# Linear attention and a gated MLP on one core: weight loads over 128 partitions, batch loads moved to SyncE, first batch rebuilt

## The chip, the cores and the metric

The kernel runs on one core of one Trainium2 chip. The metric is the time of one execution in device microseconds (us), as the median over runs. The span of a profile is about 1.8 us shorter than the time of the same run.

PE is the tensor engine, DVE the vector engine, ACT the scalar engine, POOL the GpSimd, SP (SyncE) the engine that here only issues DMAs. "ACTq" and "SPq" are the queues in which ACT and SP issue.

## The reference, cut to what matters

```python
batch, n_heads, seq, head_dim = (8, 8, 576, 64)          # q, k, v, float32
n_tokens, d_model, d_ff = (4608, 512, 2048)              # w_in 512 x 2048, w_out 2048 x 512, beta 2048

def phi(x, c, s):                                        # c, s: cos and sin of the position
    r = np.maximum(x, 0.0)
    return np.concatenate([r * c, r * s], axis=-1)
q_p, k_p = phi(q, cos_w, sin_w), phi(k, cos_w, sin_w)
kv = np.einsum('bhsf,bhsd->bhfd', k_p, v)
z = np.sum(k_p, axis=2)
num = np.einsum('bhsf,bhfd->bhsd', q_p, kv)
den = np.einsum('bhsf,bhf->bhs', q_p, z)[..., None] + 1e-06
x = num / den                                            # then the heads side by side: 4608 x 512
h = x @ w_in
out = (h * (1.0 / (1.0 + np.exp(-beta * h)))) @ w_out
```

## The kernel before

The MLP works on nine chunks of 512 tokens. Each chunk has 32 slots: 16 of `h_group` (four matmuls with w_in, then a Silu on ACT), then 16 of `o_part` (four matmuls with w_out). The attention of the next batch is worked in between the slots, so PE should never pause. Only the attention of batch 0 stands alone at the start, and all weights arrive in that time and during chunk 0.

The partition of a w_in row follows from how the attention output is turned: partition 64 jj + d of contraction block (jp, g) must hold row 256 jp + 128 jj + 64 g + d of w_in. So the 128 partitions of one block take two groups of 64 neighbouring rows, 128 rows apart. The kernel before loads each group by itself:

```python
w_in_v = moe_w_in.rearrange("(jp jj g d) f -> jj d jp g f", jp=2, jj=2, g=2)
def load_w(kind, i, f0=0, f1=512):
    ...
    for jj in range(2):                  # 64 partitions per load
        for jp in range(2):
            nc.sync.dma_start(
                out=st[jj * HP : (jj + 1) * HP, 2 * jp : 2 * jp + 2, f0:f1],
                in_=w_in_v[jj, :, jp, :, i * 512 + f0 : i * 512 + f1])
...
    for slot in range(32):               # chunk 0
        ...
    for name in "qvk":
        load_raw(2, name, eng=nc.scalar)
    for c in range(1, NTC):
        if c + 2 < B:
            for name in "qvk":
                load_raw(c + 2, name, eng=nc.scalar)     # batch loads issued by ACT
        units = att_units(c + 1) if c + 1 < B else []
```

## Time and profile before

| | before |
|---|---|
| time, median of 3 | 348.11 us (345.81 to 348.89) |
| span of the profile | 346.3 us |
| PE busy | 88% |
| mean granted clock of PE | 0.962 |
| first MLP matmul / first of chunk 1 | 25.7 / 70.1 us |

The profile page of before: the span in 40 slices of 8.7 us. The digits are tenths of busy share (PE), of full clock (PEclk) and of the 16 DMA engines' time (DMA).

```profile
PE   5469958828999899979996999899999999999994
...
PEclk9789989976999999999998999999999999999998
DMA  7999990389618942595149706960640251032022
GB/s 276 266 217 256 389 377 12 88 306 389 228 37 154 316 163 50 112 305 204 39 105 253 276 18 129 273 251 17 133 112 3 49 113 30 0 70 53 0 60 61
```

From about slice 11 on PE is nearly always busy. The loose time is mostly in the first 90 us. The DMA engines are full in slices 2 to 6, but at 217 GB/s in slice 3 and at 389 in slice 5. The windows view of before gives for each stretch (us) its length, then PE, PEld, DVE, ACT and POOL busy with counts, then the granted clock, the DMA share, GB/s:

```profile
12.00:32.00 20.00, 14.34 (x193) 8.86 (x195) 12.39 (x29) 9.29 (x16) 4.15 (x3) 0.83 1.03 212
35.00:40.00 5.00, 5.00 (x25) 2.13 (x23) 2.13 (x5) 3.90 (x6) 0.00 (x0) 1.00 1.05 388
```

The w_in loads run in the first stretch, loads of all 128 partitions in the second. Both have the engines full; the loads into 64 partitions move 212 GB/s. The Trainium skill, "SBUF — State Buffer", section "Door 1: The DMA port swizzle (why [64,N] ≈ [32,N])", says that 64 partitions reach only 8 of the 16 ports; its asymptote for them, 8 × 27.2 GB/s, is close to the 212 that this trace shows.

The PE timeline of before, MLP matmuls at the starts of chunks 0 and 1. The columns are start and duration in us, engine, line, operation, count, and in brackets the idle time before and what ended it:

```profile
25.67 14.49 PE L339 MATMUL ps<-xt,win 128*128 128x512 bf16 x64 [0.67 <-ACT xt L321]
...
70.07 1.89 PE L339 MATMUL ps<-xt,win 128*128 128x512 bf16 x8 [0.46 <-ACT xt L321]
78.83 12.75 PE L339 MATMUL ps<-xt,win 128*128 128x512 bf16 x44 [6.88 <-ACT g_t L343]
```

PE idles 6.9 us in chunk 1 because it waits for ACT (`g_t` is the Silu). What ACT did is in the timeline of all engines in that stretch:

```profile
71.37 0.79 ACTq L78 DMA_DIRECT2D raw_q<-in_q_dram  x1
72.19 3.08 ACTq L78 DMA_DIRECT2D raw_v<-in_v_dram  x1
75.31 2.74 ACTq L78 DMA_DIRECT2D raw_k<-in_k_dram  x1
...
77.14 9.66 SPq L241 DMA_TRANSPOSE qt<-qb  x1
78.09 1.27 ACT L343 ACTIVATE g_t<-ps,beta 128x512 bf16<-128x512 f32 x2 [7.59 <-issue]
```

ACT issues six batch loads in a row, two of which hold its queue for about 3 us each, and only then the Silu.

### The profile page before, as it was taken

To read this page: it belongs to the slowest core of one execution; us is meant where nothing else is said; L and a number is where in the kernel's file an instruction comes from. 1 tells how busy PE (TensorE), PEld (TensorE's weight loads), DVE (VectorE), ACT (ScalarE), POOL (GpSimd) and SP (SyncE) were. 2 spreads that over 40 slices of the span, in tenths; PEclk is the share of its full clock that TensorE was granted. 3 is DMA by queue.
4 is the path that set the end of the run, shared out by engine and by line. 5 is a ranking of instruction groups with operands and counts; after the bars stand their busy time and mean duration, and the time that the engine had idled before them with its cause. 6 is when DMAs were issued, how large, how long until landed. Compare 5 with 4: busy or idle time off the path is not lost.

```text
span 346.3 us, 5863 instructions
## 1 busy us (share of the span) xinstructions
PE 306.4 (88%) x2363; PEld 146.2 (42%) x2390; DVE 125.9 (36%) x332; ACT 136.2 (39%) x209; POOL 73.5 (21%) x83
## 2 busy tenths in 40 slices
PE   5469958828999899979996999899999999999994
PEld 2354434413444345434542444345444544444441
DVE  3871479517239024802480058114902400000000
ACT  6437501505611661256113721463166127516711
POOL 2520000310233601342131503800370120000000
PEclk9789989976999999999998999999999999999998
DMA  7999990389618942595149706960640251032022
GB/s 276 266 217 256 389 377 12 88 306 389 228 37 154 316 163 50 112 305 204 39 105 253 276 18 129 273 251 17 133 112 3 49 113 30 0 70 53 0 60 61
DMA packets 50986, 53.60 MB, mean 155 GB/s; under 512 B 31232, under 2 KB 32272, under 8 KB 50960
## 3 DMA queue, kind: packets, MB, share of 16 engines
q1 hardware_dynamic: 38736, 24.65, 28.4%
q10 hardware_dynamic: 9536, 21.24, 16.7%
q0 software_dynamic: 2688, 7.34, 9.1%
q8 instruction: 18, 0.29, 0.4%
q14 instruction: 8, 0.07, 0.1%
HBM read 36.71 MB, written 9.44 MB: 133 GB/s over the span
## 4 chain that ended last, share of the span: by engine, by line
PE 68%; DMA 17%; ACTq 5%; DVE 3%; issue 2%; SPq 2%; ACT 1%; POOL 1%; POOLq 0%; DVEq 0%
PE ps L352 32%; PE ps L339 28%; DMA w_stage<-in_moe_w_out_dram 8%; PE ps L279 5%; ACTq L78 5%; DMA qt<-qb 4%; DMA raw_k<-in_k_dram 3%; DMA w_stage<-in_moe_w_in_dram 2%; PE ps L256 2%; SPq L97 1%; DVE wout L114 1%; DVE qs L218 1%; ACT g_t L343 1%; SPq L78 1%; POOL qs L218 1%
## 5 line engine op out<-in xcount | busy, mean ns | idle before, releaser
L339 PE MATMUL ps<-xt,win 128*128 128x512 bf16 x576 | 138.4, 387 | 15.4 <-ACT g_t L343 14.3
L352 PE MATMUL ps<-wout,g_t 128*128 128x512 bf16 x550 | 126.4, 380 | 2.5 <-issue 1.6
L343 ACT ACTIVATE g_t<-ps,beta 128x512 bf16<-128x512 f32 x144 | 98.4, 687 | 61.2 <-PE ps L339 47.7
L339 PEld LDWEIGHTS <-win 128*128 128x128 bf16 x576 | 56.3, 99 | 93.4 <-issue 35.9
L352 PEld LDWEIGHTS <-g_t 128*128 128x128 bf16 x576 | 54.6, 98 | 64.8 <-issue 1.2
L366 POOL DMA_DIRECT2D out_dram<-o_sb x56 | 36.2, 650 | 167.2 <-ACT o_sb L362 167.1
L362 ACT COPY o_sb<-ps 128x512 f32<-128x512 f32 x35 | 20.5, 586 | 108.8 <-PE ps L352 108.8
L271 DVE CAST kv<-ps 64x130 bf16<-64x130 f32 x60 | 17.5, 292 | 87.8 <-PE ps L256 86.8
L218 POOL TENSOR_TENSOR qs<-qt,tanr 128x1152 bf16<-128x1152 bf16 x12 | 28.3, 2378 | 35.7 <-DMA qt<-qb 26.9
L360 DVE COPY o_sb<-ps 128x256 f32<-128x256 f32 x1 | 0.4, 425 | 65.5 <-ACT o_sb L359 65.5
L295 DVE TENSOR_TENSOR xs<-ps,rden 128x768 bf16<-128x768 f32 (+1 forms) x27 | 23.4, 868 | 0.9
L279 PE MATMUL ps<-kv,qt 128*64 128x130 bf16 x288 | 21.2, 229 | 1.3 <-DVE kv L271 1.3
L279 PE MATMUL ps<-kv,qs 128*64 128x130 bf16 x288 | 20.6, 228 | 1.1 <-DVE qs L218 0.6
L279 PEld LDWEIGHTS <-qt 128*64 128x64 bf16 x288 | 16.4, 114 | 11.3 <-issue 10.5
L256 PE MATMUL ps<-vb,rk 64*64 64x130 bf16 x576 | 12.7, 235 | 7.6 <-ACT rk L194 4.0
L214 DVE TENSOR_SCALAR vb<-raw_v,cos 128x256 bf16<-128x256 f32 x63 | 17.1, 348 | 3.4 <-DMA raw_v<-in_v_dram 3.4
L279 PEld LDWEIGHTS <-qs 128*64 128x64 bf16 x288 | 16.7, 113 | 1.4 <-DVE qs L218 0.7
L214 DVE TENSOR_SCALAR vb<-raw_v,sin 128x256 bf16<-128x256 f32 x63 | 17.1, 349 | 0.0
L290 DVE TENSOR_TENSOR den<-ps,eps 128x12 f32<-128x12 f32 (+1 forms) x27 | 4.5, 168 | 32.1 <-PE ps L279 32.1
L256 PEld LDWEIGHTS <-rk 64*64 64x64 bf16 x576 | 10.1, 116 | 12.3 <-issue 6.4
L196 DVE TENSOR_SCALAR qb<-raw_q 128x1152 bf16<-128x1152 f32 x15 | 10.7, 753 | 8.1 <-DMA raw_q<-in_q_dram 8.1
L236 ACT COPY qt<-ps 128x640 bf16<-128x640 bf16 (+1 forms) x8 | 4.9, 640 | 22.1 <-PE ps L230 17.8
(51 smaller groups left out, 79.5 us busy)
## 6 DMA issues: line engine op xcount, KB each, us to landing
out_dram<-o_sb POOLq DMA_DIRECT2D x56, 128.0 KB, 2.9
raw_q<-in_q_dram ACTq DMA_DIRECT2D x6, 1152.0 KB, 7.7
raw_v<-in_v_dram ACTq DMA_DIRECT2D x6, 1152.0 KB, 10.5
raw_k<-in_k_dram ACTq DMA_DIRECT2D x6, 1152.0 KB, 12.3
w_stage<-in_moe_w_out_dram SPq DMA_DIRECT2D x4, 1024.0 KB, 14.1
w_stage<-in_moe_w_in_dram SPq DMA_DIRECT2D x12, 256.0 KB, 9.0
out_dram<-o_sb SPq DMA_DIRECT2D x16, 128.0 KB, 2.4
raw_q<-in_q_dram SPq DMA_DIRECT2D x2, 576.0 KB, 4.5
```

What stands on the lines that cost most here:

```text
L78: (eng or nc.sync).dma_start(out=raw_tile(b, name)[:, js].rearrange("q j n d -> q j (n d)"), in_=src.rearrange("(j g) (p n) d -> (g p) j ( ...
L214: nc.vector.tensor_scalar(vb[:, n, :, cs, 0:D], rv[:, :, n, :], scalar1=t[:, n : n + 1], scalar2=None, op0=ALU.mult)
L218: eng.tensor_tensor(dst.rearrange("q n (g p) -> q n g p", g=2), src.rearrange("q n (g p) -> q n g p", g=2), tanr[:, n0:n1].unsqueeze(2).to ...
L256: nc.tensor.matmul(t[jj * HP : (jj + 1) * HP, g], lhsT=rk[hs, n, 2 * jp + jj, :], rhs=vb[hs, n, 2 * jp + jj].rearrange("q s e -> q (s e)") ...
L271: nc.vector.tensor_copy(o, a)
L279: nc.tensor.matmul(ps[gs_, bank, i * 2 * E : (i + 1) * 2 * E], lhsT=(qt, qs)[cs][:, jp, n, gs_], rhs=kv[:, g, jp, cs, :], start=(cs == 0), ...
L295: nc.vector.tensor_tensor(xs[:, jps[0] : jps[-1] + 1, 3 * t : 3 * t + 3].rearrange("q s n (j d) -> q s (n j) d", j=2), nv[:, :, :, :, 0:D] ...
L339: nc.tensor.matmul(h_ps, lhsT=win[jt // 4][:, mi, (jt % 4) * P : (jt % 4 + 1) * P], rhs=xt[:, jp, :, g * HP : (g + 1) * HP], start=(mi == ...
L343: nc.scalar.activation(g_t, h_ps, AF.Silu, scale=beta[:, jt : jt + 1])
L352: nc.tensor.matmul(o_ps, lhsT=gs[c, jt][:, tt * P : (tt + 1) * P], rhs=wout[jt // 4][:, jt % 4, :], start=(jt == 0), stop=(jt == JT - 1))
L362: nc.scalar.copy(o_sb, o_ps)
L366: eng.dma_start(out=out_v[bb, n], in_=o_sb[hf * HP : (hf + 1) * HP, :])
```

## The change

It has three parts. First, each w_in load covers all 128 partitions, to use all ports. Second, SyncE issues the batch loads, after the query transposes, so that ACT is free. Third, the attention of batch 0 is rebuilt (scaling, relu, evictions and divisions spread over DVE, ACT, POOL and PE, fewer and larger copies), and the slots of batch 1's work in chunk 0 are shifted. The diff, cut to its core:

```diff
-    w_in_v = moe_w_in.rearrange("(jp jj g d) f -> jj d jp g f", jp=2, jj=2, g=2)
+    w_in_v = moe_w_in.rearrange("(jp jj g d) f -> jp g jj d f", jp=2, jj=2, g=2)
...
-        for jj in range(2):
-            for jp in range(2):
-                nc.sync.dma_start(
-                    out=st[jj * HP : (jj + 1) * HP, 2 * jp : 2 * jp + 2, f0:f1],
-                    in_=w_in_v[jj, :, jp, :, i * 512 + f0 : i * 512 + f1])
+        for mi in range(MI):
+            nc.sync.dma_start(out=st[:, mi], in_=w_in_v[mi // 2, mi % 2, :, :, i * 512 : (i + 1) * 512])
...   (batch 0: v_scale, k_relu, kv_take, x_rden, x_mul, x_mul_act: cut)
     early = {
...
-        21: lambda: (kv_mm(1, 0, 6), kv_mm(1, 1, 6), kv_take(1, 0, 6), kv_take(1, 1, 6)),
-        22: lambda: (q_relu(1, 0), q_relu(1, 1)),
-        23: lambda: cast_w("out", 3),
-        24: lambda: q_turn_pe(1, 0, 4),
-        25: lambda: q_turn_pe(1, 1, 6),
+        22: lambda: (kv_mm(1, 0, 6), kv_mm(1, 1, 6), kv_take((0, 1), 6), q_relu(1, 0), q_relu(1, 1),
+                     q_turn_pe(1, 0, 4)),
+        23: lambda: (q_turn_pe(1, 1, 6), cast_w("out", 2)),
+        24: lambda: cast_w("out", 3),
...
+        def load_next():
+            for name in "qvk":
+                if b + 1 < B:
+                    load_raw(b + 1, name)
-            (0, lambda: (q_relu(b, 0), q_relu(b, 1))),
+            (0, lambda: (q_relu(b, 0), q_relu(b, 1), q_turn_dma(b), load_next())),
-            (1, lambda: q_turn_dma(b)),
...
-    for name in "qvk":
-        load_raw(2, name, eng=nc.scalar)
     for c in range(1, NTC):
-        if c + 2 < B:
-            for name in "qvk":
-                load_raw(c + 2, name, eng=nc.scalar)
```

The shapes of one w_in load, as built: before, source 64 × 2 × 512 (or 256) into 64 partitions; after, source 2 × 64 × 512 into 128 partitions. The first quarter, which before loads in halves, comes whole (16 loads instead of 20).

## The prediction

> **What bounds the kernel now.** The page gives PE 88% busy over a 346.3 us span, and the chain of waits is 68% PE. The steady part is bound by the tensor engine: the timeline shows about 32 us of matmuls per 512-token chunk. The loose time is at the start. By the PE timeline the first MLP matmul starts at 25.7 us and the second chunk's at 70.1 us, 44 us later where a chunk without stalls takes 32 to 33. The chain shows DMA there: w_in until 25.6 us, w_out until 51.8 us. Then ACT issues batch loads: 7 us of ACTq in the chain at 70 to 77 us (PE idles 6.9 us, released by g_t), and 1.5 to 3 us of ACTq at the start of each of chunks 2 to 5.
>
> **What the change gains.** SyncE issuing the batch loads frees ACT: I estimate 7 to 9 us in chunk 1 and 1.2 to 2 us in each of chunks 2 to 5, about 14 us. The rebuilt first batch could start the MLP some 4 us earlier, if its weights are there. Fewer and larger kv copies and transposes cost or gain nothing on the bound engine later.
>
> **What it costs: the w_in loads.** Before, each load's source pattern starts with 64 rows; the slices view shows all DMA engines busy at 200 to 240 GB/s while these run (12 to 30 us), against about 392 GB/s for the 128-partition loads. The change means to gain that factor. But in the new loads the source is a pattern of 2 x 64 x 512 (the two row groups are 128 rows apart and do not merge) against 128 partitions. The Trainium skill, "DMA: Bandwidth & Descriptors", section "Why a DMA increments its semaphore by 16 and not by 1", says a DMA from SyncE runs on the largest number of engines up to 16 that divides the outermost non-one dimension of both patterns, and takes the lowest-numbered ones. That is 2 here, the same two for all 16 loads. No load of the trace before has such a shape, so this is untested here.
>
> Estimate from the trace: 392 GB/s over 16 engines is 24.5 GB/s each (a 2 KB packet took 84 ns where ports were free). 4.19 MB over two engines takes 86 us, against about 19 us before. The first batch's loads end near 12 us, so the four w_in chunks land near 34, 55, 77 and 98 us. w_out and batch 1 wait behind them on those two engines: about 101 us for the first w_out, 106, 109 and 112 us for v, k, q, 115 and 118 us for the last w_out. Then follow the scaling of v (4.9 us), relu, the kv matmuls, the query transposes and divisions, about 21 us as before. Chunk 1 starts near 135 us instead of 70.
>
> **Sum.** 348.1 + 65 - 14 = about 399 us; I say 398 us, range 380 to 418 us. Faster by over 2%: 0.08; within 2%: 0.02; slower: 0.90.
>
> **What would show it.** w_in loads landing about 5.4 us apart; DMA busy share near 1/8 and about 50 GB/s from 12 to 98 us; PE idle in long pieces before 98 us, ended by DMA of w_stage through the casts; chunk 1 starting at 125 to 145 us; no 7 us ACTq wait after it; chunks of 32 to 34 us. A first MLP matmul near 35 us, not 25, would show the loads outweigh the rebuilt first batch.
>
> **What would make it wrong.** If the loads spread over all 16 engines, they would finish by about 23 us and the result would be near 325 us, faster by 6%. If a lone engine moves more than 24.5 GB/s, up to 10 us less; if a lone engine is slower, 10 us or more above.

## The result, and the profile after

| | before | after |
|---|---|---|
| time, median of 4 runs | 347.72 us (345.81 to 348.89) | 393.0 us (392.2 to 393.72) |
| ratio | | 1.1308 (1.125 to 1.1366) |
| span / mean granted clock | 346.3 us / 0.962 | 390.9 us / 0.899 |
| first MLP matmul / first of chunk 1 | 25.7 / 70.1 us | 34.1 / 133.8 us |
| chunks 1 to 8 and the end | 276.2 us | 257.1 us |

The last row is the span less the start of chunk 1. A ratio here is the mean time of one kernel's fast runs over that of the other's of the same rounds, so it is not quite the ratio of the medians.

The profile page of after, in slices of 9.8 us:

```profile
PE   8535032230868999999999999999999999999994
...
PEclk9755658585696999999999999999999999999999
DMA  8311111129993494890693397189064034013013
GB/s 277 130 50 52 51 51 50 50 56 292 387 389 116 94 310 152 186 377 9 131 313 151 70 237 289 22 188 365 21 136 94 2 80 90 1 27 82 1 32 77
```

For seven slices, from 20 to 88 us, the DMA engines are one or two tenths busy and move 50 to 56 GB/s, while PE mostly stands still. The windows view of after puts the share for 14 to 80 us at 0.13, about 2 of 16:

```profile
14.00:80.00 66.00, 23.58 (x169) 12.33 (x169) 8.90 (x14) 9.92 (x20) 2.02 (x2) 0.59 0.13 51
```

The PE timeline of after shows chunk 0 in four pieces, one for each quarter of w_in. Each waits 10 to 18 us for the cast of a quarter that just landed. The last line is the start of chunk 1:

```profile
34.08 5.96 PE L368 MATMUL ps<-xt,win 128*128 128x512 bf16 x16 [9.97 <-POOL win L105]
55.05 5.71 PE L368 MATMUL ps<-xt,win 128*128 128x512 bf16 x16 [15.02 <-DVE win L107]
75.86 5.54 PE L368 MATMUL ps<-xt,win 128*128 128x512 bf16 x16 [15.10 <-DVE win L107]
99.51 5.67 PE L368 MATMUL ps<-xt,win 128*128 128x512 bf16 x16 [18.10 <-DVE win L107]
...
133.80 12.06 PE L368 MATMUL ps<-xt,win 128*128 128x512 bf16 x52 [0.61 <-ACT xt L351]
```

The chain of waits of after, in the stretch from 14 to 35 us, shows loads 5.1 us apart on SP. Columns are start, duration, what.

```profile
14.03 5.07 SPq L96
...
19.14 5.08 SPq L96
...
24.26 5.08 SPq L96
```

One load is 262,144 bytes; in 5.1 us that is 51 GB/s, or 25.7 GB/s for each of two engines. SP does not wait for an earlier load here (its waits view from 4 to 82 us is empty): the issue itself takes 5.1 us, and what holds it is not shown. Two to three loads are outstanding: when the first four had landed and their cast began at 33.0 us, six had been issued and the seventh was being issued.

The w_in loads also hold up what follows them. The chain has v of batch 1 issued at 87.5 us and landing 18.8 us later:

```profile
87.49 18.81 DMA raw_v<-in_v_dram
```

The packed trace holds the time of every update of a load's semaphore. Of the sixteen for this v, fourteen came from 98.9 to 99.7 us and the last two at 106.2 and 106.3 us: its share on the two slow engines stands behind the last w_in loads and two w_out loads.

### The profile page after: what moved, and what is told of

Same layout as the page of the kernel before. It is cut to its first block, busy times and chain, and to the rows that moved or that the text cites. A ratio compares the mean times of both kernels' runs of the same rounds, so it can differ in the third digit from the quotient of the medians.

```text
span 390.9 us, 5820 instructions
## 1 busy us (share of the span) xinstructions
PE 314.0 (80%) x2398; PEld 148.4 (38%) x2398; DVE 117.5 (30%) x279; ACT 137.7 (35%) x215; POOL 74.0 (19%) x83
## 4 chain that ended last, share of the span: by engine, by line
PE 68%; SPq 22%; DMA 5%; DVE 3%; issue 1%; ACT 0%; ACTq 0%; DVEq 0%
PE ps L381 31%; PE ps L368 30%; SPq L96 19%; DMA raw_v<-in_v_dram 5%; PE ps L280 4%; PE ps L256 2%; SPq L93 2%; DVE vb L213 1%; SPq L78 1%; PE ps L228 0%; DVE qs L216 0%; DVE kv L272 0%; DVE rk L190 0%; DVE qb L190 0%; ACT g_t L372 0%
## 5 line engine op out<-in xcount | busy, mean ns | idle before, releaser
L368 PE MATMUL ps<-xt,win 128*128 128x512 bf16 x576 | 142.4, 396 | 58.9 <-DVE win L107 48.2
L381 PE MATMUL ps<-wout,g_t 128*128 128x512 bf16 x576 | 131.8, 383 | 1.9 <-DVE wout L111 1.9
L368 PEld LDWEIGHTS <-win 128*128 128x128 bf16 x576 | 57.1, 101 | 140.1 <-DVE win L107 49.7
L272 DVE CAST kv<-ps 64x520 bf16<-64x520 f32 (+1 forms) x16 | 10.6, 664 | 80.2 <-PE ps L256 80.0
L107 DVE CAST win<-w_stage 128x2048 bf16<-128x2048 f32 x3 | 3.7, 1226 | 71.1 <-DMA w_stage<-in_moe_w_in_dram 71.1
L298 DVE TENSOR_TENSOR xs<-ps,rden 128x768 bf16<-128x768 f32 x21 | 20.1, 957 | 0.7
L293 DVE TENSOR_TENSOR den<-ps,eps 128x12 f32<-128x12 f32 x21 | 3.6, 171 | 38.1 <-PE ps L280 38.1
L256 PE MATMUL ps<-vb,rk 64*64 64x130 bf16 x576 | 10.9, 224 | 3.8 <-ACT rk L188 2.6
```

Of the source, the lines that this page charges most:

```text
L256: nc.tensor.matmul(t[jj * HP : (jj + 1) * HP, g], lhsT=rk[hs, n, 2 * jp + jj, :], rhs=vb[hs, n, 2 * jp + jj].rearrange("q s e -> q (s e)") ...
L298: nc.vector.tensor_tensor(xs[:, 3 * t : 3 * t + 3].rearrange("q n s (j d) -> q s n j d", j=2), nv[:, :, :, :, 0:D], rden.unsqueeze(4).to_b ...
L368: nc.tensor.matmul(h_ps, lhsT=win[jt // 4][:, mi, (jt % 4) * P : (jt % 4 + 1) * P], rhs=xt[:, :, jp, g * HP : (g + 1) * HP], start=(mi == ...
L381: nc.tensor.matmul(o_ps, lhsT=gs[c, jt][:, tt * P : (tt + 1) * P], rhs=wout[jt // 4][:, jt % 4, :], start=(jt == 0), stop=(jt == JT - 1))
```

## The experiments

The theory (A): a DMA's engines are chosen by the outermost dimension of its patterns, and 2 in the source means two engines for all 16 loads. Rivals: (B) sixteen loads with eight in flight are limited by SyncE's waits; the chain of after does give 19% of the span to SPq L96 (though, as said above, as time of issue and not of waits). (C) Rows of 2 KB into 128 partitions are slow in themselves. The second question is what the other two parts of the change are worth, since the total hides it.

### w_in_64rows: the same loads, the outermost source dimension 64 instead of 2

Only the order of rows inside a block is changed, so that partition 2 d + jj holds what partition 64 jj + d held. The columns of the divided sums `xs` are interleaved to match, so the result is right. Count, size and issue of the loads stay. (Three patterns no longer fit in one DVE instruction, so the multiply is split in two.)

```diff
-    w_in_v = moe_w_in.rearrange("(jp jj g d) f -> jp g jj d f", jp=2, jj=2, g=2)
+    w_in_v = moe_w_in.rearrange("(jp jj g d) f -> jp g d jj f", jp=2, jj=2, g=2)
...
-        nc.vector.tensor_tensor(
-            xs[:, 3 * t : 3 * t + 3].rearrange("q n s (j d) -> q s n j d", j=2), ...)
+        for s in range(2):
+            nc.vector.tensor_tensor(
+                xs[:, 3 * t : 3 * t + 3, s].rearrange("q n (d j) -> q n j d", j=2), ...)
```

> The kernel after, with the same 16 w_in loads of 256 KB into all 128 partitions, but the source pattern turned from 2 x 64 x 512 to 64 x 2 x 512 (the columns of the divided sums are interleaved to match, so the result stays right). Theory A, engines are set by the outermost dimension of the source (2 after, 64 here, so 16 engines): w_in streams at about 390 GB/s and is in by about 23 us, the first MLP matmul starts at about 25 us, chunk 1 at about 58 us, time about 323 us (316 to 332), 17% faster than after. Theory B, the loads are slow because there are 16 of them with eight in flight and SyncE waiting for each: nothing changes, 393 us. Theory C, 2 KB rows into 128 partitions are slow: 393 us.

Measured: correct, 327.12 us (323.92 to 328.74), ratio to before 0.9382 (0.9316 to 0.9448). That is 66 us less than after. The first MLP matmul is at 23.3 us (A expected about 25); chunk 1 starts at 65.1 us, later than the 58 us expected. B and C fall: the loads have the same number, size, row length, number of partitions, queue and programmed waits.

### outer4 and outer8: two more points of the same curve

The source is regrouped as 4 × 32 × 512 and 8 × 16 × 512; the rows go to the wrong partitions, so the result is wrong.

```diff
-    w_in_v = moe_w_in.rearrange("(jp jj g d) f -> jp g jj d f", jp=2, jj=2, g=2)
+    w_in_v = moe_w_in.rearrange("(a mi r) f -> mi a r f", a=4, mi=4)      # or a=8
```

> The kernel after, w_in source pattern 4 x 32 x 512 (the rows go to the wrong partitions, so the result is wrong on purpose). Theory A: four engines, about 98 GB/s, 43 us for w_in instead of 86, loads 2.7 us apart, time about 350 us (343 to 358). Theories B and C: 393 us.

> The kernel after, w_in source pattern 8 x 16 x 512 (wrong result on purpose). Theory A: eight engines, about 196 GB/s, 21 us for w_in, time about 330 us (323 to 338). Theories B and C: 393 us.

Measured in one look each (one run, state unknown): 354.52 and 334.42 us, and wrong results as intended. The windows view from 14 to 22 us, of outer4, outer8 and w_in_64rows in this order; the last two numbers of each line are the DMA share and GB/s:

```profile
14.00:22.00 8.00, 4.80 (x144) 4.15 (x134) 6.14 (x11) 2.91 (x11) 0.00 (x0) 1.00 0.27 103
```

```profile
14.00:22.00 8.00, 5.33 (x137) 4.80 (x125) 5.46 (x10) 2.09 (x7) 2.02 (x2) 0.79 0.54 204
```

```profile
14.00:22.00 8.00, 5.71 (x120) 4.93 (x120) 5.60 (x10) 2.62 (x9) 2.02 (x2) 0.79 1.04 385
```

With after's line the curve is complete: outermost source dimension 2, 4, 8, 64 gives 51, 103, 204, 385 GB/s and a DMA share of 0.13, 0.27, 0.54, 1.04. The rate is about 25 GB/s per engine and the number of engines is 2, 4, 8, 16. The semaphore updates in the packed traces give the same numbers without any rate: when a w_in load lands, its semaphore is updated 2 times in after, 4 in outer4, 8 in outer8 and 16 in w_in_64rows. The share also shows that the loads use the same engines: two to three are outstanding in after, and if each took another pair, the share would not stay at 2 of 16.

### old_w_in: after with the w_in loads of before

```diff
-        for mi in range(MI):
-            nc.sync.dma_start(out=st[:, mi], in_=w_in_v[mi // 2, mi % 2, :, :, i * 512 : (i + 1) * 512])
+        (the w_in_v and the loads of before, 64 partitions each)
```

> The kernel after with the w_in loads of before (20 loads into 64 partitions each, first chunk in halves). Theory A: the 86 us of w_in go back to about 19 us and what remains is the gain of the other two parts: about 332 us (326 to 340), 4 to 6% faster than before. If the rest of the change also costs something, 348 us or more.

Measured: 329.62 us (328.48 to 330.53), ratio 0.9457 (0.9415 to 0.95). So the rest of the change is worth 5.4%, and the new loads alone turned that into a loss.

### new_w_in_only: before with the new w_in loads alone

> The kernel before with the new w_in loads alone (source 2 x 64 x 512). If they alone cost what the prediction says, +65 us less the part hidden by nothing: about 410 us (400 to 420). If the cost needs the rebuilt first batch or the SyncE batch loads, under 390 us.

The edit is the first two hunks of the change's diff (with the first quarter whole). Measured: correct, 413.65 us (409.49 to 414.11), ratio 1.1919 (1.1813 to 1.2024). Chunk 1 starts at 133.8 us, exactly where after has it. The loads cost 66 us alone, and 63 us with the other two parts around them (393.0 us of after against 329.62 of old_w_in).

### sync_only and first_batch_only: the other two parts alone

sync_only is before with the second part: the hunks with `load_next` and without `eng=nc.scalar`, and batch 2's loads at slot 24.

> The kernel before with one part of the change: the batch loads of batches 2 and up are issued by SyncE, behind the query transposes, instead of by ACT. If ACT's issuing stalls the MLP (the prediction), the 6.9 us of PE idle at 72 us and the 1 to 3 us at the start of chunks 2 to 5 go: 12 us less, about 336 us (331 to 341). If these waits were slack that something else would fill: 346 us or more.

Measured: 328.34 us (327.11 to 328.95), ratio 0.9477 (0.9413 to 0.9542), a better result than the range expected. The timeline of sync_only at the start of chunk 1:

```profile
70.23 10.20 PE L339 MATMUL ps<-xt,win 128*128 128x512 bf16 x44 [0.46 <-ACT xt L321]
...
70.70 4.03 SPq L241 DMA_TRANSPOSE qt<-qb  x1
...
76.60 4.72 POOL L218 TENSOR_TENSOR qs<-qt,tanr 128x1152 bf16<-128x1152 bf16 x2 [5.43 <-DVE vb L214]
```

There is no pause between the MLP groups. The query transpose now stands ahead of the batch loads and holds SP for 4.0 us instead of 9.7, so POOL starts on its result (`qs`) at 76.6 us. Batch 2's loads are also issued earlier here: in before DVE had waited 6.5 us for `raw_q` ahead of that transpose. The two effects are not separated. In before the line reads:

```profile
92.66 4.72 POOL L218 TENSOR_TENSOR qs<-qt,tanr 128x1152 bf16<-128x1152 bf16 x2 [22.18 <-DMA qt<-qb]
```

first_batch_only has the third part: after with w_in loads and batch loads as before.

> The kernel after with w_in loads and batch loads as before; the rebuilt first batch and the shifted slots of chunk 0 remain. old_w_in less the gain of the SyncE loads: about 341 us (336 to 346), 2% faster than before, first MLP matmul at 24 us against 25.7. If the first batch brings all of old_w_in's gain: 330 us.

Measured: 344.02 us (342.49 to 345.51), ratio 0.9934 (0.9854 to 1.0014), not clear of no change. The first MLP matmul came at 25.8 us, not the expected 24.

### idle_filled: is the clock's drop to half after the pause part of the cost?

In before the records of the granted clock show half clock for 10.2 us from 74.1 us on, 2 us into the pause, and the 44 MLP matmuls behind it took 12.75 us (10.20 in sync_only). Dummy matmuls fill the pause:

```diff
                 h_group(c, slot)
+                if c == 1 and slot == 1:
+                    warm_pe(28, bank=5)
```

> The kernel before with 28 matmuls on zeros into an unused PSUM bank after the second MLP group of chunk 1, where PE sat idle 6.9 us (about 6 us of filler). If the idle time itself makes the clock drop to half afterwards, the 44 MLP matmuls behind the wait take 10.3 us instead of 12.75, chunk 1 is about 2.5 us shorter (40 us instead of 42.6) and the time about 345.5 us. If the half clock has another cause, or the filler delays the MLP: no change or slower.

Measured: 344.34 us (342.92 to 345.99), ratio 0.9926 (0.9885 to 0.9967). The PE timeline of idle_filled, with the filler (L371), the MLP behind it, a later wait and what followed it:

```profile
72.98 6.21 PE L371 MATMUL ps<-zeros 128*128 128x512 bf16 x28
80.09 10.26 PE L339 MATMUL ps<-xt,win 128*128 128x512 bf16 x44 [0.91 <-ACT g_t L343]
...
98.76 0.25 PE L279 MATMUL ps<-kv,qs 128*64 128x130 bf16 x2 [1.80 <-POOL qs L218]
...
99.17 3.41 PE L352 MATMUL ps<-wout,g_t 128*128 128x512 bf16 x8
```

The first half of the expectation held: the matmuls took 10.26 us, so the pause did bring the half clock. The second half fell: chunk 1 was not shorter (44.4 us against 42.6). PE then waited for `qs`, which is late because the query transpose comes behind the batch loads, and after that wait half clock was recorded for 3.4 us from 99.4 us (8 matmuls in 3.41 us, 1.90 in before). The filler took away the half clock after ACT's stall, not the stall itself and not the late transpose; taking that half clock away alone gave nothing in this chunk. The small gain in total is not from chunk 1; in this one profile chunk 4 was 3.6 us shorter, and why stays open.

### w64_early_q, and a comparison on one chip

In w_in_64rows chunk 0 took 41.8 us (23.3 to 65.1). Its PE timeline shows two pauses:

```profile
47.34 0.68 PE L228 MATMUL ps<-ident,qb 128*128 128x128 bf16 x9 [2.38 <-DVE qb L190]
...
51.91 4.46 PE L382 MATMUL ps<-wout,g_t 128*128 128x512 bf16 x12 [1.91 <-DVE wout L111]
```

Both wait for DVE, and DVE had been idle just before (DVE timeline of w_in_64rows, the eviction of kv):

```profile
45.08 1.41 DVE L272 CAST kv<-ps 64x520 bf16<-64x520 f32 x2 [5.28 <-PE ps L256]
```

The relu of the queries and a weight cast are moved into that idle time (both at once; neither was run alone):

```diff
         19: lambda: k_relu(1),
-        22: lambda: (kv_mm(1, 0, 6), kv_mm(1, 1, 6), kv_take((0, 1), 6), q_relu(1, 0), q_relu(1, 1),
-                     q_turn_pe(1, 0, 4)),
-        23: lambda: (q_turn_pe(1, 1, 6), cast_w("out", 2)),
+        20: lambda: (q_relu(1, 0), q_relu(1, 1)),
+        21: lambda: cast_w("out", 2),
+        22: lambda: (kv_mm(1, 0, 6), kv_mm(1, 1, 6), kv_take((0, 1), 6), q_turn_pe(1, 0, 4)),
+        23: lambda: q_turn_pe(1, 1, 6),
```

> The kernel of w_in_64rows, with the relu of batch 1's queries moved ahead of its kv matmuls (slot 20) and the third w_out cast to slot 21. There PE idled 2.4 us for qb and 1.9 us for wout in chunk 0 while DVE idled 5.3 us just before. If nothing else takes their place, chunk 1 starts near 61 us instead of 65 and the time is about 4 us less than that run: 321 to 324 us. If the loads land too late for those slots, no gain.

Measured: correct, 318.6 us (317.99 to 319.55), ratio 0.9206 (0.9132 to 0.928), better than expected. The same lines in the PE timeline of w64_early_q have no pause:

```profile
45.80 0.68 PE L228 MATMUL ps<-ident,qb 128*128 128x128 bf16 x9
...
47.95 2.75 PE L382 MATMUL ps<-wout,g_t 128*128 128x512 bf16 x12
```

The 12 matmuls took 2.75 us instead of 4.46. The granted clock of the profile page, w_in_64rows first, then w64_early_q, accounts for it. The 5 in the seventh slice of the first (48 to 56 us) is the half clock that followed the pauses:

```profile
PEclk9889995999999999999999999999999999999999
```

```profile
PEclk9998999999999999999999999999999999999999
```

sync_w64 is before with the SyncE loads and the w_in loads of w_in_64rows, without the rebuilt first batch.

> The kernel before with two parts: the batch loads on SyncE (as in sync_only) and the w_in loads of w_in_64rows (source 64 x 2 x 512, 16 engines); the first batch and the slots of chunk 0 stay as before. If the rebuilt first batch earns its keep once the weights are early, this is 2 us or more above w_in_64rows, 329 us or more; if it earns nothing, about 325 to 327 us. Chunk 0 (25.7 to 70.2 us in sync_only) shows it directly.

> The kernel of w_in_64rows once more, on the same chip as sync_w64 and the next run, because its times ranged over 5 us (324 to 329) in a call of its own. 324 to 329 us again; chunk 0 from 23.3 to 65.1 us.

> The kernel of w64_early_q beside w64_again on one chip. If the moved relu and cast save PE's two idle pieces in chunk 0 (4.3 us) and also keep the clock from dropping to half there (6.8 us at half speed in w_in_64rows, worth up to 3.4 us), the difference is 5 to 8 us: 318 to 320 us. If only the idle pieces count: 4 us.

| | time, median of 6 | ratio to before (95%) | first MLP matmul | chunk 0 |
|---|---|---|---|---|
| sync_w64 | 322.61 us | 0.9298 (0.9261 to 0.9334) | 25.9 us | 39.2 us |
| w64_again | 327.77 us | 0.9428 (0.9373 to 0.9483) | 22.8 us | 42.9 us |
| w64_early_q_again | 319.68 us | 0.9214 (0.9177 to 0.9251) | 24.3 us | 37.1 us |

sync_w64 was faster than both answers that had been foreseen. The third part of the change starts the MLP 3.1 us sooner (22.8 against 25.9 us), but its shifted slots make chunk 0 3.8 us longer, and w64_again was 1.6% slower than sync_w64 (327.77 / 322.61). With the relu and the cast moved, chunk 0 is 37.1 us, and the kernel with the rebuilt first batch is 2.9 us ahead of sync_w64 (0.9%; the slots of sync_w64 were not tuned in the same way, so what the rebuilt first batch is worth by itself stays open). Between w64_again and w64_early_q_again there are 8.1 us, at the top of the 5 to 8 expected; their profiled spans differ by 4.3 us (322.8 and 318.5). In w64_again the half clock was recorded for 6.8 us from 49.0 us; neither sync_w64 nor w64_early_q_again has one near there. Part of the difference in time between these runs (5.2 us between sync_w64 and w64_again, against 0.7 us in their profiled spans, 322.1 and 322.8) varies from run to run and is not explained by one profile: w64_again's runs ranged from 324.56 to 329.12 us.

## Why the prediction was right

It said 398 us, between 380 and 418, and slower with a chance of 0.90; 393.0 us was measured. Point by point:

- **Two engines.** Right. Predicted about 50 GB/s and a DMA share near 1/8; measured 51 GB/s and 0.13. This rested on the Trainium skill, "DMA: Bandwidth & Descriptors", section "Why a DMA increments its semaphore by 16 and not by 1" (the largest number up to 16 that divides both outermost dimensions). The page agrees with four points here: 2, 4, 8 and 64 gave 2, 4, 8 and 16 engines' worth of rate, and as many semaphore updates per load.
- **The rate of one engine.** Taken from before's trace as 24.5 GB/s, which gave loads 5.4 us apart; they were 5.1 us apart, 25.7 GB/s.
- **The arrivals.** The four quarters were expected near 34, 55, 77 and 98 us. The casts that waited for them began at 33.0, 53.8, 74.6 and 98.2 us. The last hit is in part luck: the loads came faster than predicted (20.8 us from quarter to quarter), but the last quarter took 23.6 us, with w_out loads already issued from 81.3 us on; why it took longer was not tested. v of batch 1 was expected at 106 us and landed at 106.3.
- **Chunk 1.** Expected near 135 us, measured 133.8, and the chunks after it take 32.5 us each without an ACTq wait (32 to 34 were expected). The first MLP matmul was expected near 35 us and measured at 34.1.
- **The gain of the other parts.** Mis-sized. The prediction took 14 us off for the SyncE loads; the time from chunk 1 to the end fell by 276.2 − 257.1 = 19.1 us, and sync_only alone gave 346.3 − 328.2 = 18.1 us (means). Chunk 1 fell by 10.1 us (42.6 to 32.5), and chunks 2 to 5 by 1.2, 2.5, 4.5 and 1.1 us, where 1.2 to 2 each was expected. The 14 us are what PE stood idle for the Silu in before, by its waits view (us in total, times, longest):

```profile
PE ps L339 <- ACT g_t L343: 14.3, 5, 6.9
```

  What the term left out is the half clock after a pause: 2.5 us in chunk 1 (12.75 − 10.20) and 1.6 us in chunk 4 (a pause of 2.8 us and then 44 matmuls in 11.87 us instead of 10.26). It also left out the transposes behind the batch loads, on whose result PE waits next in idle_filled.
- **The rebuilt first batch.** The prediction gave it "some 4 us earlier, if its weights are there" and no term in the sum. In after the weights were not there. Where they were, the MLP started 1.6 to 3.1 us earlier than in sync_w64, but the shifted slots of w64_again spent it again.

The sum with measured terms, 348.1 + (133.8 − 70.1) − 19.1 = 392.7 us, meets the profiled run (392.64 us) by construction, since the terms are stretches of the two profiles. It shows where the forecast of 399 us was off by 6 us: 5.1 us are the SyncE term and 1.3 us the loads (63.7 us instead of 65).

The intent of the first part was sound: 128 partitions moved 385 GB/s, against 212 for 64. Its gain could show only with a source pattern that gives all 16 engines, and it is small then: w_in_64rows against old_w_in, in one call, is 327.12 against 329.62 us, with intervals of the two ratios that overlap; sync_w64 against sync_only, in two calls, has the ratios 0.9298 and 0.9477 to before, clear of each other.

## What to carry to other kernels

Before you widen a DMA, look at the outermost dimension of both its patterns as built, not only at the number of partitions: two separate row groups folded into one load put it on two engines, and everything queued behind it on those engines waits too. If the rows must be gathered from two places, make the large dimension the outer one and interleave the layout of the other operand to match. When a change has several parts, run each alone: here one part hid a gain of 5%, and a second (the rebuilt first batch) was not clear of no change alone and came out 0.9% ahead only after two instructions had been moved into idle time.

## What the Trainium skill lacked or had wrong

- "DMA: Bandwidth & Descriptors", section "Rules for kernel authors": the row on two transfers to disjoint partition halves says to use one 128-partition transfer instead. Here the one transfer, with a source of 2 × 64 rows, moved 51 GB/s and the half transfers 212 GB/s. That row does not point to the row "Use all 16 engines", which states what went wrong.
- The same page gives about 27 GiB/s for one engine (section "Specifications"), which is 29 GB/s; 25 to 26 GB/s per engine were measured on two, four and eight. It has no number for the loads behind a load on few engines: a 1152 KB load of all engines landed 18.8 us after its issue, with its share on the two slow engines in line behind the last w_in loads and two w_out loads.
- "TensorE: Matmul & The Clock Gate", section "Part 1: The HAM clock gate (the "warmup" mystery)", gives half clock after at least one idle window of about 3.4 us. Here less idle time was enough: in before half clock was recorded from 74.1 us on, 2.1 us after the last matmul, and in w_in_64rows for 6.8 us from 48.6 us on, after one pause of 2.4 us (45.0 to 47.3 us) and before the next, of 1.9 us. Its second profile (w64_again) shows the same, and neither profile of w64_early_q, without the pauses, does. It is no fixed length either: a pause of 2.4 us in chunk 3 of before (up to 150.7 us) brought none.
- No page says how long an issue of a batch load or a transpose can hold its engine's queue when other loads are in flight: 3.1 us for one of ACT's loads, 5.1 us for a w_in load on two engines (0.6 us in before), and 9.7 us for a transpose behind the batch loads against 4.0 us ahead of them.
